# The product with w_out by one level of Strassen over pairs of batches

## The chip, the cores and the metric

The kernel runs on one core of a Trainium2 chip. The metric is the device time of one execution in microseconds, the median of three runs. The engines are named as in the profile: PE is the matrix engine (TensorE), PEld its loading of weights, DVE is VectorE, ACT is ScalarE, POOL is GpSimd; SP is SyncE, which issues most of the transfers, in order.

## What is computed

Three layers follow on each other for 4 batches (B) of 448 tokens (S) and 768 columns (DM): sigmoid attention over 12 heads, a layer with a spatial gate, and a layer that mixes tokens by a complex rotation. The change lies in the second one:

```python
h = np.maximum(x @ w_in, 0.0)                  # 768 -> 1024
u, v = h[..., :512], h[..., 512:]
v_n = (v - mu) / np.sqrt(var + 1e-06)          # over the 512 columns
v_s = np.einsum('ts,bsd->btd', w_spatial, v_n) + b_spatial[None, :, None]
gated = u * v_s
x = gated @ w_out                              # 512 -> 768, goes into the third layer
# third layer
theta = x @ w_theta
y = einsum(w_tok_r, x * cos(theta)) + einsum(w_tok_i, x * sin(theta))
u = x + y
out = u + np.maximum(u @ w_ch, 0.0)
```

## The kernel before, in words

Every product is taken in split precision. A value is kept as a high part, rounded to the matrix engine's format, and a low part, the rest; `mm3` sums three matmuls (high by high, high by low, low by high) into PSUM. Making such a pair takes a copy on ACT (`acopy`) for the high part and a subtraction on DVE (`sub`) for the low part.

The program runs through these stages. **Attention**: 24 rounds in an order that is written out by hand for PE, ACT, DVE and SP. Beside them the weights of the later layers are read, put together from 64-bit values and written back to device memory as 32-bit ones (`Piece`; `f_out` is w_out, `f_th` w_theta, `f_tok` the token weights, `f_ch` w_ch). **First product** (`uv(b, g)`): eight groups for a batch, four for v (`g < 4`) and four for u; each is reduced in a PSUM tile `psd`, copied by ACT with a relu to `ev`, and stored to `v_d` and `u_d`. Some groups run among the rounds, the last ten behind them (`while todo`). The fourth group of v holds the last 64 tokens of two batches. **Spatial product** (`spatial(b, n)`): for each of four chunks `f` of 128 columns of v it makes 11 matmuls into a tile `psp`, multiplies that by the chunk of u on DVE (`gf`, L499) and splits the result into `g`. **Product with w_out** (`project(b, G, d, ps)`): for each of six blocks `d` of 128 output columns, four chunks of 128 of the 512 inner columns times three matmuls into a tile `ppo`; ACT copies it to `x2` and stores it to `x_d`. **Third layer**: the product with w_theta (`pt`), the rotation, the mixing (`py`), and at the end the product with w_ch, which already has the seven-product form that the change brings to w_out (L887).

`ln(b)` loads v of a batch in three transfers (the first 384 tokens, and twice the last 64), takes mean and variance (`bn_stats`, `bn_aggr` on DVE, a power on POOL), scales v on DVE (L468), and splits it into `vh` and `vl`. `prep` loads blocks of a weight into `wq` and splits them. Behind the attention rounds a scheduler sets the order in which each engine's instructions stand; an engine takes its own in that order. PE there has: ten `psd` groups, the spatial products of batches 0 and 1, w_out for batch 0, spatial 2, w_out 1, spatial 3, w_out 2 and 3, theta. PSUM has eight banks; the spatial and the w_out tiles share one pool of six (`ps_2`).

Of the kernel before, what the change touches and what calls it, by code (L numbers as in the profile page):

```python
# [20 lines left out]
DM, DFF = 768, 1024  # L21
# [30 lines left out]
def net(ctx: ExitStack, tc: tile.TileContext, kq, vd, vl, w_in, w_sp, bsp, w_out, w_th, w_tok, w_ch, out):  # L52
# [12 lines left out]
    def mm3(ps, wh, wl, xh, xl, first, last):  # L65
        te.matmul(ps, wh, xh, start=first, stop=False)  # L66
        te.matmul(ps, wh, xl, start=False, stop=False)  # L67
        te.matmul(ps, wl, xh, start=False, stop=last)  # L68

    const = ctx.enter_context(tc.tile_pool(name="const", bufs=1))  # L70
    dram = ctx.enter_context(tc.tile_pool(name="dram", bufs=1, space=DRAM))
# [178 lines left out]
        ve.tensor_copy(xl[b // 2, p][:, :, b % 2, :], X[:, :, L0:S].bitcast(F32))  # L250
        xs[b, p] = X

    def uv(b, g):
        ps = banks("psd")[:, 0, :]
        if g < 4:
            for k in range(KC):
                if g < 3:
                    xh, xlo = (xs[b, k][:, i, g * P:(g + 1) * P] for i in range(2))
                else:
                    xh, xlo = (xl[b // 2, k][:, i].rearrange("p b t -> p (b t)") for i in range(2))  # L260
                te.matmul(ps, xh, wih[:, k, DH:], start=k == 0, stop=False)  # L261
                te.matmul(ps, xh, wil[:, k, DH:], start=False, stop=False)  # L262
                te.matmul(ps, xlo, wih[:, k, DH:], start=False, stop=k == KC - 1)  # L263
            r = x_p.tile([P, DH], F32, tag="ev", name="ev", bufs=2)
            acopy(r, ps, AF.Relu)
            if g < 3:
                nc.scalar.dma_start(v_d[b][g * P:(g + 1) * P, :], r)
            else:
                nc.scalar.dma_start(v_d[b - 1][L0:S, :], r[0:64])
                nc.scalar.dma_start(v_d[b][L0:S, :], r[64:P])  # L270
        else:
            f = g - 4
            fs = slice(f * P, (f + 1) * P)
            for k in range(KC):
                X = xs[b, k]
                mm3(ps[:, :S], wih[:, k, fs], wil[:, k, fs], X[:, 0, :], X[:, 1, :], k == 0, k == KC - 1)
            r = x_p.tile([P, DH], F32, tag="ev", name="ev", bufs=2)
            acopy(r[:, :S], ps[:, :S], AF.Relu)
            nc.scalar.dma_start(u_d[b][fs, :], r[:, :S])

    class Piece:

# [82 lines left out]
    with tc.manual_schedule(engines={mybir.EngineType.PE, mybir.EngineType.Activation, mybir.EngineType.DVE, mybir.EngineType.SP}):  # L365
# [71 lines left out]
        while pieces or loaded or apart or joined:  # L437
            begin_pieces(2)
            end_pieces()
    es_l.close()  # L440


    es_w = ExitStack()
    wb_p = es_w.enter_context(tc.tile_pool(name="wb", bufs=1, reuse_waits="tile"))
    NB = FC * DM + 4 * S
    wbh = wb_p.tile([P, NB], F32R, tag="wbh", name="wbh")
    wbl = wb_p.tile([P, NB], F32R, tag="wbl", name="wbl")
    sph, spl = (w[:, FC * DM:].rearrange("p (c t) -> p c t", c=4) for w in (wbh, wbl))
    woh, wol = (w[:, :FC * DM].rearrange("p (c f) -> p c f", c=FC) for w in (wbh, wbl))
    pxa = es_w.enter_context(tc.tile_pool(name="pxa", bufs=1, reuse_waits="tile"))  # L450
    es_a = ExitStack()
    pw = es_a.enter_context(tc.tile_pool(name="pw", bufs=2, reuse_waits="tile"))
    def ln(b):
        v = pa.tile([P, 4, DH], F32, tag="v", name="v")
        nc.sync.dma_start(v[:, 0:3, :], v_d[b][0:L0, :].rearrange("(c p) f -> p c f", p=P))
        nc.sync.dma_start(v[0:64, 3, :], v_d[b][L0:S, :])
        nc.sync.dma_start(v[64:P, 3, :], v_d[b][L0:S, :])
        st = pa.tile([P, 4, 6], F32, tag="st", name="st")
        mv = pa.tile([P, 4, 2], F32, tag="mv", name="mv")
        for c in range(4):  # L460
            ve.bn_stats(st[:, c, :], v[:, c, :])
            ve.bn_aggr(mv[:, c, :], st[:, c, :])
        ve_ = pa.tile([P, 4], F32, tag="ve", name="ve")
        ve.tensor_scalar_add(ve_, mv[:, :, 1], EPS)
        rs = pa.tile([P, 4], F32, tag="rs", name="rs")
        nc.gpsimd.tensor_tensor(out=rs, in0=ve_, in1=mhalf, op=ALU.pow)
        for c in range(4):
            ve.tensor_scalar(out=v[:, c, :], in0=v[:, c, :], scalar1=mv[:, c, 0:1], scalar2=rs[:, c:c + 1],  # L468
                             op0=ALU.subtract, op1=ALU.mult)
        vh = pa.tile([P, 4, DH], F32R, tag="vh", name="vh")  # L470
        vl = (p2 if b % 2 else pa).tile([P, 3, DH], F32R, tag="vl", name="vl", bufs=1)
        acopy(vh, v)
        sub(vl, v[:, 0:3, :], vh[:, 0:3, :])
        sub(vh[64:P, 3, :], v[64:P, 3, :], vh[64:P, 3, :])
        acopy(vb[b % 2][0:64], v[0:64, 3, :])
        return vh, vl

    U = {}

    def load_u(b):  # L480
        for f in range(FC):
            u = U[b, f] = pa.tile([P, S], F32, tag="u", name="u", bufs=4)
            nc.sync.dma_start(u, u_d[b][f * P:(f + 1) * P, :])

    def spatial(b, n):
        vh, vl = n
        G = []
        for f in range(FC):
            fs = slice(f * P, (f + 1) * P)
            ps = ps_2.tile([P, 512], F32, tag="d", name="psp")  # L490
            o = ps[:, :S]
            for c in range(3):
                te.matmul(o, vh[:, c, fs], sph[:, c, :], start=c == 0, stop=False)
                te.matmul(o, vh[:, c, fs], spl[:, c, :], start=False, stop=False)
                te.matmul(o, vl[:, c, fs], sph[:, c, :], start=False, stop=False)
            te.matmul(o, vh[:, 3, fs], sph[:, 3, :], start=False, stop=False)
            te.matmul(o, vb[b % 2][:, fs], spl[:, 3, :], start=False, stop=True)
            gf = p2.tile([P, S], F32, tag="gf", name="gf")
            ve.tensor_tensor(out=gf, in0=o, in1=U.pop((b, f)), op=ALU.mult)  # L499
            g = pg.tile([P, 2, S], F32R, tag="g", name="g", bufs=6)  # L500
            acopy(g[:, 0, :], gf)
            sub(g[:, 1, :], gf, g[:, 0, :])
            G.append(g)
        return G

    NAMES = ("A11", "A12", "S2", "S1", "S3", "S4", "A22")
    KH = KC // 2
    SUMS = ("S3", "S4")
    f_s = dram.tile([P, KH, len(SUMS), HALF], F32, name="f_s")

    def project(b, G, d, ps):
        ds = slice(d * P, (d + 1) * P)
        for f in range(FC):
# [14 lines left out]
    for i in range(2):  # L528
# [2 lines left out]
        for r in (64, 96):  # L531
            nc.gpsimd.memset(t[r:r + 1].bitcast(F32), 1.0)
        vb.append(t)
    prep(pw, sph, spl, w_sp, 4)
    br = pw.tile([P, S], F32, name="br", bufs=1)
    for r in (64, 96):
        nc.sync.dma_start(br[r:r + 1], bsp)
    bh = pw.tile([P, S], F32R, name="bh", bufs=1)
    nc.gpsimd.memset(spl[64:P, 3, :].bitcast(F32), 0.0)
    ve.tensor_copy(spl[64:65, 3, :], br[64:65])  # L540
    ve.tensor_copy(bh[96:97], br[96:97])
    sub(spl[96:97, 3, :], br[96:97], bh[96:97])
    n0 = ln(0)
    load_u(0)
    prep(pw, woh, wol, f_out, FC)
    while todo:
        uv(*todo.pop(0))
    es_ps.close()
    es_r.close()


    es_ps = ExitStack()
    ps_2 = es_ps.enter_context(tc.tile_pool(name="ps_2", bufs=6, space=PSUM, reuse_waits="tile"))
# [15 lines left out]
    p2 = es_a.enter_context(tc.tile_pool(name="p2", bufs=2, reuse_waits="tile"))  # L569
    G = None  # L570
    for b in range(B):
        Gn = spatial(b, n0)
        if b + 1 < B:
            load_u(b + 1)
            n0 = ln(b + 1)
        if b == 0:
            prep(pw, thh, thl, f_th, KC)
        if b == 1:
            prep(pw, tkh, tkl, f_tok, 7)
        if G is not None and b + 1 < B:  # L580
            for d in range(KC):
                project(b - 1, G, d, ps_2.tile([P, 512], F32, tag="d", name="ppo"))
        if b + 1 < B:
            G = Gn
        else:
            halve(0)
    es_a.close()


    pxb = es_w.enter_context(tc.tile_pool(name="pxb", bufs=2, reuse_waits="tile"))  # L590
    es_b = ExitStack()
    pb = es_b.enter_context(tc.tile_pool(name="pb", bufs=2, reuse_waits="tile"))
# [49 lines left out]
    load_x(0)  # L642
    for n in steps[:2]:
        part_planes(*n)
    split_x(*steps[0])
    join_planes(*steps[0])
    se.activation(warm, XR[steps[0]][:, 0:4], AF.Sin, scale=0.0)
    for b, g in ((B - 2, G), (B - 1, Gn)):
        for d in range(KC):
            project(b, g, d, ps_2.tile([P, 512], F32, tag="d", name="ppo"))  # L650
    es_g.close()
    es_ps.close()

# [147 lines left out]
    with tc.manual_schedule(engines={mybir.EngineType.SP}):  # L801
        for b in range(B):
            for i in range(4):
                for h in range(2):
# [20 lines left out]
                    if i < 3 and (i or b == 2):  # L825
# [175 lines left out]
```

## Time and profile before

| | before |
|---|---|
| median of three runs | 618.04 us (617.21 to 618.92) |
| the profiled execution, first to last instruction | 616.3 us |
| PE busy | 610.3 us (99%) |
| loading of weights on PE | 508.6 us (83%) |
| DVE busy | 414.7 us (67%) |
| ACT busy | 347.2 us (56%) |
| granted clock of PE, mean | 1.000 |

The page of the profile gives the span of the profiled execution alone; the median of the runs is 1.7 us above it. An engine's busy share is a mean over all stages. It doesn't tell whether another engine ever waits for it, nor, for PE, whether a matmul is at its peak, since matmuls overlap and their recorded ends are modelled.

### The profile page before, as it was taken

What the parts mean: (1) busy time and instruction counts of PE and PEld (TensorE: products, weight loads), DVE (VectorE), ACT (ScalarE), POOL (GpSimd) and SP (SyncE); (2) the same over time, 40 slices, a digit from 0 to 9 for tenths busy, and PEclk for the clock granted to TensorE, in tenths of its full rate; (3) what the DMA queues carried; (4) which work ended last, traced back from release to release, by engine and by line L of the source; (5) the groups of instructions that cost most, each with busy time, mean ns of one, the idle gap of its engine ahead of it and who ended that gap; (6) DMA issues with size and microseconds to landing.
All of it is one profiled execution on the core that took longest, in us unless ns stands there. A gap on an engine that the chain in (4) does not pass through costs nothing.

```text
span 616.3 us, 9173 instructions
## 1 busy us (share of the span) xinstructions
PE 610.3 (99%) x3302; PEld 508.6 (83%) x3302; DVE 414.7 (67%) x824; ACT 347.2 (56%) x589; POOL 8.1 (1%) x18
## 2 busy tenths in 40 slices
PE   9999999999999999999999999999999999999997
PEld 4547666856776689999999999999999999999996
DVE  4788577626753557795231497797587787887875
ACT  6896766554656325346236396677376574562540
POOL 0000000000000110000000000000000000000000
PEclk9999999999999999999999999999999999999999
DMA  8758589749864597675867612472085026153503
GB/s 306 275 205 265 180 296 293 243 155 308 271 209 158 178 282 245 192 215 167 224 198 234 188 39 78 90 243 65 27 215 171 26 99 223 60 189 118 213 33 133
DMA packets 83106, 112.62 MB, mean 183 GB/s; under 512 B 27890, under 2 KB 69748, under 8 KB 83060
## 3 DMA queue, kind: packets, MB, share of 16 engines
q1 hardware_dynamic: 74964, 99.00, 50.9%
q10 hardware_dynamic: 8096, 13.03, 6.0%
q8 instruction: 26, 0.43, 0.3%
q14 instruction: 20, 0.16, 0.1%
HBM read 68.06 MB, written 32.93 MB: 164 GB/s over the span
## 4 chain that ended last, share of the span: by engine, by line
PE 93%; DVE 3%; DMA 1%; ACT 1%; issue 1%; SPq 0%; DVEq 0%
PE psa L235 7%; PE py L725 6%; PE py L726 6%; PE py L727 5%; PE pss L206 5%; PE pt L685 5%; PE pt L686 5%; PE pt L684 5%; PE psd L261 3%; PE ppo L67 3%; PE ppo L66 3%; PE ppo L68 3%; PE psd L263 3%; PE psd L262 3%; PE psd L66 3%; PE psd L68 3%
## 5 line engine op out<-in xcount | busy, mean ns | idle before, releaser
L192 ACT ACTIVATE af<-pss,bias 128x896 f32<-128x896 f32 x72 | 66.1, 1022 | 4.9 <-PE pss L202 3.1
L685 PE MATMUL pt<-thl,XT 128*128 128x384 f32 x168 | 56.9, 338 | 0.0
L235 PE MATMUL psa<-af,vr 128*64 128x448 f32 x288 | 56.8, 543 | 0.0
L686 PE MATMUL pt<-thh,XT 128*128 128x384 f32 x168 | 56.8, 338 | 0.0
L684 PE MATMUL pt<-thh,XT 128*128 128x384 f32 x168 | 56.7, 338 | 0.0
L235 PEld LDWEIGHTS psa<-af,vr 128*64 128x64 f32 x288 | 19.6, 137 | 36.3 <-issue 34.7
L63 ACT ACTIVATE ev<-psd 128x448 f32<-128x448 f32 (+1 forms) x30 | 17.0, 567 | 47.5 <-PE psd L263 22.8
L112 DVE SCALAR_TENSOR_TENSOR wq<-wraw,wq 128x384 int32<-128x384 int32 (+2 forms) x51 | 28.7, 594 | 20.7 <-ACT wraw L107 20.6
L66 PE MATMUL psd<-X,wih 128*128 128x448 f32 x96 | 35.7, 372 | 0.0
L68 PE MATMUL psd<-X,wil 128*128 128x448 f32 x96 | 35.2, 367 | 0.2 <-DVE wil L57 0.2
L57 DVE TENSOR_TENSOR X<-psa,X 128x448 fp32r<-128x448 f32 x24 | 14.6, 623 | 30.9 <-ACT X L63 30.9
L67 PE MATMUL ppo<-g,wbh 128*128 128x448 f32 x96 | 35.2, 366 | 0.0
L66 PE MATMUL ppo<-g,wbh 128*128 128x448 f32 x96 | 35.1, 366 | 0.0
L68 PE MATMUL ppo<-g,wbl 128*128 128x448 f32 x96 | 35.1, 366 | 0.0
L67 PE MATMUL psd<-X,wih 128*128 128x448 f32 x96 | 35.1, 366 | 0.0
L107 ACT ACTIVATE wraw<-wraw 128x384 f32<-128x384 f32 (+2 forms) x51 | 29.4, 604 | 9.6 <-DVE wq L100 7.0
L695 ACT ACTIVATE m<-r 128x384 f32<-128x384 f32 x28 | 14.7, 524 | 33.1 <-DVE r L693 33.1
L685 PEld LDWEIGHTS pt<-thl,XT 128*128 128x128 f32 x168 | 31.5, 188 | 0.4
L684 PEld LDWEIGHTS pt<-thh,XT 128*128 128x128 f32 x168 | 31.5, 188 | 0.4
L102 DVE SCALAR_TENSOR_TENSOR wq<-wraw,wq 128x384 int32<-128x384 int32 (+2 forms) x51 | 30.6, 600 | 1.8
L686 PEld LDWEIGHTS pt<-thh,XT 128*128 128x128 f32 x168 | 31.5, 188 | 0.0
L261 PE MATMUL psd<-wih,X 128*128 128x512 f32 x72 | 28.4, 394 | 0.0
(292 smaller groups left out, 1570.3 us busy)
## 6 DMA issues: line engine op xcount, KB each, us to landing
kqr<-in_kq SPq DMA_DIRECT2D x23, 448.0 KB, 4.9
wraw<-in_w_in SPq DMA_DIRECT2D x12, 512.0 KB, 6.1
x_d<-x ACTq DMA_DIRECT2D x24, 224.0 KB, 3.3
xb<-x_d SPq DMA_DIRECT2D x4, 1344.0 KB, 7.4
xp<-xa SPq DMA_DIRECT2D x56, 96.0 KB, 2.5
y_d<-y SPq DMA_DIRECT2D x24, 224.0 KB, 2.0
out_t<-o SPq DMA_DIRECT2D x23, 224.0 KB, 1.9
vr<-in_vd SPq DMA_DIRECT2D x24, 192.0 KB, 5.0
```

The lines of the kernel that those rows point to most:

```text
L66: te.matmul(ps, wh, xh, start=first, stop=False)
L67: te.matmul(ps, wh, xl, start=False, stop=False)
L68: te.matmul(ps, wl, xh, start=False, stop=last)
L192: se.activation(af, ps[:, :, :S], AF.Sigmoid, bias=bias, scale=1.0 / math.sqrt(D))
L206: te.matmul(ps[:, j, :S], t[w][a, 0, c], t[x][a, 1, :], start=n == 0, stop=n == 2)
L235: te.matmul(ps[a, :S], t["v"][:, 2 * c + j, :], t["a"][c][:, j, :], start=False, stop=c == 2)
L261: te.matmul(ps, xh, wih[:, k, DH:], start=k == 0, stop=False)
L684: te.matmul(o, t[:, k, 0, :], thh[:, k, hs], start=k == 0, stop=False)
L685: te.matmul(o, t[:, k, 0, :], thl[:, k, hs], start=False, stop=False)
L686: te.matmul(o, t[:, k, 1, :], thh[:, k, hs], start=False, stop=k == KC - 1)
L725: te.matmul(o, z[:, 0, ds], tkh[:, c, :], start=i == 0 and n == 0, stop=False)
L726: te.matmul(o, z[:, 0, ds], tkl[:, c, :], start=False, stop=False)
```

## The change

Two batches are taken as one pair, b and b+1. Write the gated values, with the 512 inner columns halved, as y0[0], y0[1] (batch b) and y1[0], y1[1] (batch b+1), and w_out as four blocks: rows halved like the inner columns, columns halved at 384. One level of Strassen (in Winograd's form) then takes seven block products instead of eight, of the weights A11, A12, S2, S1, S3, S4, A22 (S1 to S4 are sums of blocks) with B11, B21, T2, T1, T3, B22, T4, in this order on PE. B11 and B21 are the halves of batch b, B22 is one of batch b+1, and T1 to T4 are the differences that four DVE instructions make, in place of the gated values. Each product runs over three blocks `d` of 128 columns, two chunks `c` and three matmuls. Some products are accumulated in a bank that holds an earlier one; others are copied out by ACT (`kept`) and added on DVE to what has been kept (`plus`), which also stores the result through SP.

Around it:
- `spatial` writes its products over u, which is loaded in two transfers a batch into six buffers (`pu`).
- `Norm` scales v on ACT instead of DVE. v of batch 1 is loaded to a place of its own.
- `OutPart` loads the four blocks of one chunk of w_out, splits three, makes S1 to S4 on DVE (four instructions of 384 columns), and splits those. There are two of them.
- The PSUM pools `ps_2` (five banks, with the spatial product) and `ps_a` (three) are opened before the last ten groups of the first product, which use them (`uv_last`).
- Both spatial products of a pair come ahead of its w_out product. The weights of theta and of the token mixing are split at other places, two of them by way of arguments of `project`.
- In the last stage one of the steps that sum w_ch's blocks comes earlier, and the scratch size of the transfers is set.

```diff
 def spatial(b, n):
...
-            gf = p2.tile([P, S], F32, tag="gf", name="gf")
-            ve.tensor_tensor(out=gf, in0=o, in1=U.pop((b, f)), op=ALU.mult)
-            g = pg.tile([P, 2, S], F32R, tag="g", name="g", bufs=6)
-            acopy(g[:, 0, :], gf)
-            sub(g[:, 1, :], gf, g[:, 0, :])
-            G.append(g)
-        return G
+            u = U[b, f // GH][:, f % GH, :]
+            marks['y'] = ve.tensor_tensor(out=u, in0=o, in1=u, op=ALU.mult).ins
+        return [U.pop((b, j)) for j in range(2)]
...
-    def project(b, G, d, ps):
-        ds = slice(d * P, (d + 1) * P)
-        for f in range(FC):
-            mm3(ps[:, :S], woh[:, f, ds], wol[:, f, ds], G[f][:, 0, :], G[f][:, 1, :], f == 0, f == FC - 1)
-        r = pg.tile([P, S], F32, tag="x2", name="x2", bufs=3)
-        acopy(r, ps[:, :S])
-        nc.scalar.dma_start(x_d[b][ds, :], r)
+    def project(b, y0, y1, early, beside):
+        def half(y):
+            t = pg.tile([P, 2, GH, S], F32R, tag="g", name="g", bufs=3)
+            marks['g'] = acopy(t[:, 0], y).ins
+            sub(t[:, 1], y, t[:, 0])
+            return t
...
+        B11, B21 = half(y0[0]), half(y0[1])
+        marks.update({'ya': marks['y'], 'ga': marks['g']})
+        t = pu.tile([P, GH, S], F32, tag="u", name="t1")
+        sub(t, y1[0], y0[0])
+        sub(y0[0], y1[1], t)
+        A = [ps_a.tile([P, 512], F32, tag="a", name="pa_") for d in R3]
+        for d in R3:
+            out_product(A[d], "A11", B11, d, True)
+        p1 = [kept(A[d]) for d in R3]
+        T2 = half(y0[0])
+        E = [ps_2.tile([P, 512], F32, tag="d", name="pb_") for d in R3]
+        for d in R3:
+            out_product(E[d], "A12", B21, d, True)
+            plus(E[d], p1[d], b, d)
+        T1 = half(t)
+        early()
+        sub(y1[0], y1[1], y1[0])
+        sub(y0[1], y0[1], y0[0])
+        for d in R3:
+            out_product(A[d], "S2", T2, d, False)
+        u2 = [kept(A[d]) for d in R3]
+        T3 = half(y1[0])
...
+    with tc.issue_after(last_uv.ins):
+        y0 = spatial(0, N[0])
+        y1 = spatial(1, N[1])
+    project(0, y0, y1, lambda: N.update({2: ln(2)}), lambda: None)
+    load_u(2)
+    N[3] = ln(3)
+    y0 = spatial(2, N[2])
+    load_u(3)
+    with tc.issue_after(marks['ya']), tc.issue_after(marks['ga']):
+        prep(pw, thh, thl, f_th, KC)
+    y1 = spatial(3, N[3])
```

DVE's instructions from the second spatial product on, before. Here `gf` is a gated chunk, `g` its split form, `thl` the low part of w_theta, `vl` and `vh` those of v:

```order
L57 TENSOR_TENSOR g<-gf,g 128x448
L57 TENSOR_TENSOR thl<-wq,thh 128x384 x2
L499 TENSOR_TENSOR gf<-psp,u 128x448 x2
L57 TENSOR_TENSOR vh<-v,vh 64x512
L57 TENSOR_TENSOR g<-gf,g 128x448 x2
L57 TENSOR_TENSOR thl<-wq,thh 128x384 x2
L499 TENSOR_TENSOR gf<-psp,u 128x448 x2
```

The same place in the changed kernel, in the first pair, from the first low half of the gated values (`g<-u`) to that of T2 (the last row). `u<-psp,u` are the multiplies, `t_2714` is T1, and `u<-u` are the sums made in place:

```order
L57 TENSOR_TENSOR g<-u,g 128x896
L525 TENSOR_TENSOR u<-psp,u 128x448
L57 TENSOR_TENSOR g<-u,g 128x896
L57 TENSOR_TENSOR t_2714<-u 128x896
L525 TENSOR_TENSOR u<-psp,u 128x448
L57 TENSOR_TENSOR vh<-v,vh 64x512
L57 TENSOR_TENSOR wtkl<-wq,wtkh 128x448
L525 TENSOR_TENSOR u<-psp,u 128x448
L57 TENSOR_TENSOR thl<-wq,thh 128x384
L57 TENSOR_TENSOR u<-u,t_2714 128x896
L57 TENSOR_TENSOR u<-u 128x896 x2
L57 TENSOR_TENSOR g<-u,g 128x896
```

Each chunk was split on its own behind its multiply; now the sums of both batches stand between the last multiply and the split of T2, with pieces of the second batch pair's v (`vh`) and of later weights (`wtkl`, `thl`) among them.

SP's transfers in the attention rounds, as the difference of the two kernels. `wo` is the staging of `OutPart`, `wraw` a raw weight, `kqr` queries and keys:

```order
 L91 DMA wraw_1096<-in_w_th 128x384
 L91 DMA wraw_1098<-in_w_th 128x384
-L299 DMA f_out_99<-wq_1090 128x384
-L299 DMA f_th_100<-wq_1093 128x384
+L542 DMA wo_2274<-f_out_99 128x384
+L542 DMA wo_2341<-f_out_99 128x384
+L301 DMA f_out_99<-wq_1090 128x384
+L301 DMA f_th_100<-wq_1093 128x384
 L91 DMA wraw_1138<-in_w_th 128x384
 L91 DMA wraw_1140<-in_w_th 128x384
+L542 DMA wo_2341<-f_out_99 128x384
 L175 DMA kqr_1177<-in_kq 128x896
 L175 DMA kqr_1179<-in_kq 128x896
```

Loads of w_out's blocks, which stood behind the rounds, now stand between its stores and the next loads of weights, queries and keys.

## Rows read from the trace of the kernel before

**Rows 1.** The page, first part: busy time of each engine, share of the span, instructions.

```profile
span 616.3 us, 9173 instructions
...
PE 610.3 (99%) x3302; PEld 508.6 (83%) x3302; DVE 414.7 (67%) x824; ACT 347.2 (56%) x589; POOL 8.1 (1%) x18
```

**Rows 2.** The view of waits of PE: in total, times, longest, all in us.

```profile
PE pss L372 <- DVE idle L369: 1.1, 1, 1.1
PE pss L206 <- ACT af L192: 0.8, 2, 0.6
```

**Rows 3.** Windows (us): PE, PEld, DVE, ACT, POOL busy, granted clock, DMA share, GB/s.

```profile
210.60:248.90 38.30, 38.30 (x181) 33.71 (x180) 26.03 (x60) 15.67 (x25) 5.68 (x10) 1.00 0.75 236
...
248.90:343.90 95.00, 95.00 (x468) 87.58 (x467) 44.19 (x77) 42.73 (x74) 2.05 (x2) 1.00 0.69 206
```

**Rows 4.** Timeline of PE around 249 and 343 us: start, duration, instruction.

```profile
249.11 0.36 PE L493 MATMUL psp<-wbh,vh 128*128 128x448 f32 x1
...
343.45 0.37 PE L68 MATMUL ppo<-g,wbl 128*128 128x448 f32 x1
```

**Rows 5.** One tile's instructions, ppo: durations in ns, first and last start.

```profile
L66 PE MATMUL ppo<-g,wbh x96: 358/367/373, 267.0 to 343.0; 128*128 128x448 f32 x96
```

**Rows 6.** Groups of DVE by form: busy us, mean ns of one, idle before.

```profile
L57 DVE TENSOR_TENSOR kql<-kqr,kqh 128x896 fp32r<-128x896 f32 x23 | 25.1, 1092 | 0.8
...
L461 DVE BATCH_NORM_STATS2 st<-v 128x6 f32<-128x512 f32 x16 | 10.3, 675 | 0.8 <-DMA v<-v_d 0.8
...
L499 DVE TENSOR_TENSOR gf<-psp,u 128x448 f32<-128x448 f32 x16 | 9.5, 616 | 0.0
...
L468 DVE TENSOR_SCALAR v<-v,mv,rs 128x512 f32<-128x512 f32 x16 | 7.7, 544 | 4.4 <-POOL rs L466 4.4
L57 DVE TENSOR_TENSOR vl<-v,vh 128x1536 fp32r<-128x1536 f32 x4 | 7.0, 1752 | 3.2 <-ACT vh L63 3.2
...
L57 DVE TENSOR_TENSOR thl<-wq,thh 128x384 fp32r<-128x384 f32 x12 | 6.3, 552 | 1.3 <-ACT thh L63 1.3
...
L57 DVE TENSOR_TENSOR wtkl<-wq,wtkh 128x448 fp32r<-128x448 f32 x7 | 4.4, 625 | 11.9 <-ACT wtkh L63 11.9
...
L57 DVE TENSOR_TENSOR vh<-v,vh 64x512 fp32r<-64x512 f32 x4 | 2.8, 690 | 0.1
```

**Rows 7.** Groups of ACT by form, the same columns.

```profile
L192 ACT ACTIVATE af<-pss,bias 128x896 f32<-128x896 f32 x72 | 66.1, 1022 | 4.9 <-PE pss L202 3.1 <-PE pss L206 1.8
...
L63 ACT ACTIVATE ev<-psd 128x512 f32<-128x512 f32 x14 | 8.4, 597 | 23.2 <-PE psd L263 22.8 <-ACT ev L63 0.5
...
L63 ACT ACTIVATE vh<-v 128x2048 fp32r<-128x2048 f32 x4 | 7.6, 1904 | 4.4 <-DMA wq<-f_out 4.4
...
L63 ACT ACTIVATE wbh<-wq 128x384 fp32r<-128x384 f32 x8 | 4.0, 520 | 6.3 <-DMA wq<-f_out 6.3
```

**Rows 8.** Timeline around 210 us, where the last ten groups begin.

```profile
209.98 0.62 DVE L57 TENSOR_TENSOR X<-psa,X 128x448 fp32r<-128x448 f32 x1 [0.48 <-ACT X L63]
...
210.61 0.47 PE L66 MATMUL psd<-X,wih 128*128 128x448 f32 x1
```

**Rows 9.** Timeline of SP in the attention rounds.

```profile
97.75 0.33 SPq L299 DMA_DIRECT2D f_out<-wq  x1
...
102.62 0.33 SPq L175 DMA_DIRECT2D kqr<-in_kq  x1
```

**Rows 10.** DMA issues: KB each, median us from issue to landing.

```profile
u<-u_d SPq DMA_DIRECT2D x16, 224.0 KB, 3.8
...
f_out<-wq SPq DMA_DIRECT2D x8, 192.0 KB, 3.6
...
v<-v_d SPq DMA_DIRECT2D x8, 128.0 KB, 4.0
...
v_d<-ev ACTq DMA_DIRECT2D x4, 128.0 KB, 4.3
```

**Rows 11.** Timeline of ACT's queue: the last store of v.

```profile
236.39 0.49 ACTq L269 DMA_DIRECT2D v_d<-ev  x1
```

More of the change, by code (lines that the diff above doesn't have):

```diff
@@ L67, in mm3 @@
         te.matmul(ps, wh, xl, start=False, stop=False)
-        te.matmul(ps, wl, xh, start=False, stop=last)
+        return te.matmul(ps, wl, xh, start=False, stop=last)
     const = ctx.enter_context(tc.tile_pool(name="const", bufs=1))
@@ L279, in uv @@
             nc.scalar.dma_start(u_d[b][fs, :], r[:, :S])
+        return ins
     class Piece:
@@ L478, in net @@
+    def ln(b):
+        n = Norm(b)
+        n.stats()
+        n.scale()
+        n.split()
+        return n
     U = {}
     def load_u(b):
-        for f in range(FC):
-            u = U[b, f] = pa.tile([P, S], F32, tag="u", name="u", bufs=4)
-            nc.sync.dma_start(u, u_d[b][f * P:(f + 1) * P, :])
+        for j in range(2):
+            u = U[b, j] = pu.tile([P, GH, S], F32, tag="u", name="u")
+            nc.sync.dma_start(u, u_d[b][j * GH * P:(j + 1) * GH * P, :].rearrange("(c p) t -> p c t", p=P))
@@ L509, in net @@
     f_s = dram.tile([P, KH, len(SUMS), HALF], F32, name="f_s")
[L511 to L517 removed]
+    WO = {n: [w[:, i] for w in (woh, wol)] for i, n in enumerate(("A11", "A12", "A22", "S3", "S2", "S4", "S1"))}
@@ new lines, in net, with out_product, kept, put @@
+    marks = {}
+    def project(b, y0, y1, early, beside):
[4 more added lines that the diff above has]
+            return t
+        def out_product(ps, n, Y, d, first):
+            ds = slice(d * P, (d + 1) * P)
+            h, l = WO[n]
+            for c in range(GH):
+                for i, (w, j) in enumerate(((h, 0), (h, 1), (l, 0))):
+                    te.matmul(ps[:, :S], w[:, c, ds], Y[:, j, c, :], start=first and c == 0 and i == 0,
+                              stop=c == GH - 1 and i == 2, skip_group_check=not first)
+        def kept(ps):
+            r = pg.tile([P, S], F32, tag="x2", name="x2", bufs=8)
+            acopy(r, ps[:, :S])
+            return r
+        def put(q, i, d, r):
+            q.dma_start(x_d[i][d * P:(d + 1) * P, :], r)
+        def plus(ps, r, i, d):
+            add(r, ps[:, :S], r)
+            put(nc.sync, i, d, r)
+        R3 = range(KH)
+        B11, B21 = half(y0[0]), half(y0[1])
[20 more added lines that the diff above has]
+        T3 = half(y1[0])
+        E = [ps_2.tile([P, 512], F32, tag="d", name="pe_") for d in R3]
+        for d in R3:
+            out_product(E[d], "S1", T1, d, True)
+        p5 = [kept(E[d]) for d in R3]
+        B22 = half(y1[1])
+        for d in R3:
+            out_product(A[d], "S3", T3, d, False)
+            plus(A[d], p5[d], b + 1, d + KH)
+        T4 = half(y0[1])
+        beside()
+        for d in R3:
+            out_product(E[d], "S4", B22, d, False)
+            plus(E[d], u2[d], b + 1, d)
+        for d in R3:
+            out_product(A[d], "A22", T4, d, False)
+            put(nc.scalar, b, d + KH, kept(A[d]))
@@ L568, in net @@
     pg = es_g.enter_context(tc.tile_pool(name="pg", bufs=2, side="right", reuse_waits="tile"))
[L569 to L586, printed above, removed]
+    pu = es_g.enter_context(tc.tile_pool(name="pu", bufs=6, side="right", reuse_waits="tile"))
+    load_u(0)
+    load_u(1)
+    with tc.issue_after(last_uv.ins):
[9 more added lines that the diff above has]
+    y1 = spatial(3, N[3])
     es_a.close()
+    pxa = es_w.enter_context(tc.tile_pool(name="pxa", bufs=1, reuse_waits="tile"))
+    halve(0)
     pxb = es_w.enter_context(tc.tile_pool(name="pxb", bufs=2, reuse_waits="tile"))
@@ L644, in net, with begin_theta @@
         part_planes(*n)
[L645 to L650, printed above, removed]
+    def begin_theta():
+        split_x(*steps[0])
+        join_planes(*steps[0])
+        se.activation(warm, XR[steps[0]][:, 0:4], AF.Sin, scale=0.0)
+    project(2, y0, y1, lambda: prep(pg, tkh, tkl, f_tok, 7), begin_theta)
     es_g.close()
```

144 lines of the change are left out of this document (96 added, 48 removed).

## The prediction

> **What bounds the kernel now.** I read the busy times first. TensorE (PE) is busy for 610.3 of the 616.3 us [rows 1], so the reader should ask next whether any other engine is ever waited for. The view of PE's waits answers it: its largest entries are 1.1 us at the very start and 0.8 us in two pieces [rows 2], both far ahead of the part that is changed. The windows then show that part: from 248.9 to 343.9 us (the spatial product and the product with w_out) PE is busy for all 95.00 us at a granted clock of 1.00, VectorE (DVE) for 44.19, ScalarE (ACT) for 42.73 [rows 3]. So a matmul taken out of this stage shortens the run by its place in PE's stream, as long as what feeds the rest stays in time.
>
> That place is read from starts, not from durations. The first spatial matmul starts at 249.11, the last one of the w_out product at 343.45 [rows 4]. Between them lie 16 groups of 11 spatial matmuls and 24 groups of 12 for w_out, 464 in all, so (343.45 - 249.11) / 463 = 0.2038 us from one to the next. The recorded duration of one is 367 ns [rows 5]: neighbours overlap, and durations would count each column of time nearly twice.
>
> **What is removed.** Before, the product needs 4 batches x 6 column blocks x 4 chunks x 3 = 288 matmuls. After, each of two batch pairs needs 7 products x 3 blocks x 2 chunks x 3 = 126, in all 252. 36 x 0.2038 = **7.34 us** less. Against the profiled span that is 616.3 - 7.3 = 609.0; the median of the runs is 618.04, 1.7 us above that span, and I carry this offset along: 618.04 - 7.34 = 610.7 if nothing waits.
>
> The Trainium skill ("TensorE: Matmul & The Clock Gate", section "Back-to-back issue gap") gives a warm matmul N / 2.4 GHz plus about 2.5 ns, for 448 columns 189 ns. By it the gain is an estimated 36 x 0.189 = 6.8 us. The starts above say 204, so the measured pitch stands.
>
> **What is added on DVE.** Prices are those of like forms [rows 6]: 1.092 us for a subtraction over 128x896, 0.616 for one over 128x448 out of PSUM. Low halves: 14 x 1.092 in place of 16 of half the size, 15.3 - 9.9 = +5.4. Block sums: 8 x 1.092 = +8.7. Adds of a product to a kept one: 18 x 0.616 = +11.1. The scaling of v goes to ACT: 16 x 0.544 = -8.7. Sum +16.5, so about 61 of the remaining 87.7 us. On ACT the high halves are at most 14 x 1.022 us more [rows 7], about 57 of 87.7. Neither becomes the bound by its sum. The 8 block sums and 6 more blocks of w_out lie before 248.9, where DVE is busy for 26.03 and ACT for 15.67 of 38.3 us [rows 3]; they cost nothing while that idle time covers them, and at most a late start of the spatial product if not.
>
> The scaling on ACT has no row: 128x512 with two per-row operands. The bounds are 0.597 (a copy of 128x512) and 1.022 (128x896 with one such operand) [rows 7]; being nearest in size to the former I take 0.7. The Trainium skill ("ScalarE: Activation LUTs") has 280 ns + 0.833 ns a column with a pointer operand and some 93 ns for a second, an estimated 0.80 us here; no run so far shows it, and it speaks against the move by 0.4 us for a batch of four.
>
> **Where PE can now be made to wait.** The excerpt of DVE's order shows it. In the first pair PE runs the 44 spatial matmuls of batch 1, then A11 and A12 (36), and then S2, which needs T2, the third sum split. In DVE's row T2 stands behind batch 2's normalised v, and its high half may be written only when batch 0's spatial product is through. From that moment: ACT's copy 1.904 [rows 7]; then on DVE [rows 6] vl 1.752, four multiplies 4 x 0.616, two low halves 2 x 1.092, one sum 1.092, vh 0.690, one block each of two weights 0.625 and 0.552, three sums 3 x 1.092, T2's low half 1.092: 13.7 us. Together 15.6. PE has (44 + 36) x 0.2038 = 16.3 us of work. The margin is 0.7 us; handing over from ACT to DVE and from DVE to PE is not in it (0.01 us from the end of a read to PE's start in [rows 8]). I take a wait of 0.3 us, with nothing and 1 us as bounds. In the second pair only a multiply, three sums and the low half, 5.0 us, face the 36 x 0.2038 = 7.3 us of A11 and A12: no wait.
>
> **The handover ahead of it.** The last products of the first layer now use the new PSUM pools, whose first bank is free when DVE has read X. That read starts at 209.98 and takes 0.62, and PE starts at 210.61 because of it already [rows 8]. I take 0.1, at most one more such read, 0.6.
>
> **SyncE's queue (SP) in the attention rounds.** Eight loads of w_out's blocks and three of v now stand there, as the second excerpt shows; each w_out load waits until its store has landed, 3.6 us [rows 10]. The store is issued at 97.75, so the load holds SP until about 101.4; its next own wait, a load of queries and keys, is issued at 102.62 [rows 9]. So I take 0.1. If a landing takes twice as long, 7.2, SP is free at 105.3 only, 2.7 us too late, and the splits of queries and keys that PE's scores wait for are late by as much: 2.7 is the upper bound, nothing the lower.
>
> Moving the other preparations and one step of the last stage changes no count on PE, and the same idle time of DVE and ACT hides it. Sum: -7.34 + 0.3 + 0.1 + 0.1 = -6.84, **611.2 us**.
>
> **Rivals.**
> *T2 late because of batch 2's statistics* (chance 0.18). The last rows of v for batch 2 are stored by ACT, at 236.39 before [rows 11], land 4.3 later, and are loaded in 4.0 [rows 10]: 244.7. Statistics 4 x 0.675 and four scalings bring it to about 251 to 254, against 249.1 + 44 x 0.204 = 258.1, when the copy may start anyway: 4 us to spare or more. For it speaks that the scaling of batches 0 and 1 (8 x 0.6 to 1.0) and six more blocks of w_out (6 x 0.520 = 3.1) now stand ahead of that store on ACT, 8 to 11 us; against it that ACT is idle for 22.6 of the 38.3 us around. If all of it delays the store, PE loses up to 7 us, if the idle time takes most of it, none. Between, 2.5: 618.04 - 7.34 + 2.5 = 613.2.
>
> *SP's queue late in the rounds* (0.06): 610.7 + 2.7 = 613.4.
>
> *The durations are right after all* (0.03): 36 x 0.367 = 13.2, 604.8. Against it stands that 464 x 0.367 = 170 us do not fit into 95. The Trainium skill's "Trainium Kernel Development and Optimization" calls matmul busy time a bad metric since matmuls are pipelined; by that rule, the trace agrees.
>
> *The gain is eaten* (0.08): the rival on batch 2 at its full 7 us, 617.7, no change that can be told.
>
> *Slower* (0.05). The load of batch 2's last rows on SP waits for the store, and the loads of the gated half u stand behind it. If they are late, no spatial product can be multiplied, the five banks fill, and PE stops. The store's 4.3, u's 3.8 [rows 10] and a multiply of 0.6 must be over by 249.1 + 5 x 11 x 0.204 = 260.3, so the store may leave at 251.6. Before it left at 236.39, 15 us earlier. A loss begins there, and the run is slower than before by over 0.3% (1.85 us, about what a measurement of this kernel can tell from no change) only from 15 + 7.3 + 1.9 = 24 us of delay. Delayed by 30 us, it would end at 624.
>
> **How the numbers follow.** The likeliest case, waits of 0 to 1 us plus the small terms, has 0.60 and reaches from 610.0 to 612.5. Below it the durations' case holds 0.03, above it the waits of 1 to 4 us 0.24. The range from 609.7 to 614.6 takes in the bounds of T2 and SP and leaves the eaten gain, the slower case and the durations' case out. Faster: 0.60 + 0.03 + nearly all of 0.24, 0.86; same 0.09; slower 0.05.
>
> **What the profile after would show.** Right: the matmuls from the first spatial one to the last of w_out number 428 and keep a pitch of 0.204, so about 87.2 us; PE's waits there sum to under 1 us; what there is stands at S2 of the first pair and is put down to DVE's split of T2; the attention rounds have the waits of before. Wrong would be the prediction if PE waits for several us at S2 or at the later products behind ACT's or DVE's splits, if the first layer's products or the rounds grow longer, or if the stage that follows starts later than the stage that precedes it has become shorter.

## The result, and the profile after

The changed kernel took 612.71 us, the median of four runs (612.18 to 613.15), beside 618.13 for the kernel before (four runs, 617.21 to 618.92). The ratio is 0.9914, with a 95% interval from 0.99 to 0.9928. The forecast was 611.2, with a range from 609.7 to 614.6: the time lies in it, and 1.5 us above the number.

The page of the profiled execution, its first part:

```profile
span 611.2 us, 9106 instructions
...
PE 603.5 (99%) x3266; PEld 501.8 (82%) x3266; DVE 437.9 (72%) x840; ACT 363.2 (59%) x599; POOL 9.9 (2%) x18
```

PE is still busy for nearly all of the span, which is 5.1 us shorter [rows 1]. The next view is the waits of PE; they are to be read beside [rows 2]:

```profile
PE pss L206 <- ACT af L192: 1.7, 1, 1.7
PE pss L374 <- DVE idle L371: 1.1, 1, 1.1
PE pe__3285 L574 <- DVE g L57: 0.7, 1, 0.7
PE pss L202 <- DMA kqr<-in_kq: 0.3, 1, 0.3
```

The wait of 1.1 us at the start is that of before. New is an entry on `pe__3285`, a bank of the product with w_out, and the wait for ACT's `af`, early in the attention rounds, has grown from 0.8 to 1.7. The windows of the three stretches from the last ten groups of the first product on (the same columns as in [rows 3]) show where the time went:

```profile
211.70:250.20 38.50, 38.50 (x182) 33.92 (x181) 29.86 (x56) 22.51 (x29) 7.28 (x9) 1.00 0.43 139
250.20:338.76 88.56, 87.80 (x430) 80.26 (x428) 62.57 (x97) 51.69 (x79) 2.23 (x2) 1.00 0.71 221
338.76:611.20 272.44, 268.99 (x1387) 254.17 (x1385) 210.45 (x436) 154.81 (x300) 0.00 (x0) 1.00 0.41 125
```

Three differences of starts make up the 5.1 us:

| stretch | before | after | difference |
|---|---|---|---|
| start to the first spatial matmul | 249.11 [rows 4] | 250.20 | +1.09 |
| from there to the start of the last w_out matmul | 94.34 [rows 4] | 88.35 | -5.99 |
| from there to the end | 272.85 | 272.67 | -0.18 |

The stretch that is changed gave 5.99 instead of 7.34 us. The 1.35 us are in PE's timeline (start, duration, instruction; in brackets idle time and its releaser), in the second pair:

```profile
328.65 0.36 PE L574 MATMUL pa__3169<-g,wbl 128*128 128x448 f32 x1
329.12 0.67 PE L574 MATMUL pa__3170<-g,wbh 128*128 128x448 f32 x2
...
330.44 0.41 PE L574 MATMUL pe__3285<-g,wbh 128*128 128x448 f32 x1
331.51 0.47 PE L574 MATMUL pe__3285<-g,wbh 128*128 128x448 f32 x1 [0.66 <-DVE g L57]
```

The starts of neighbours lie 0.204 apart elsewhere. From 328.65 to 329.12 it is 0.47, from 330.44 to 331.51 it is 1.07, and the start behind each such wait comes 0.1 later than the pitch: 0.26 + 0.11 + 0.87 + 0.11 = 1.35. The reader should ask what ACT and DVE did just then. ACT's timeline (`g` is the high part of an operand of the product, `x` a copy out of PSUM; `XT`, `xr` and the table load are theta's first step, the beginning of the next layer):

```profile
316.03 0.94 ACT L63 ACTIVATE g<-t 128x896 fp32r<-128x896 f32 x1
321.98 1.59 ACT L63 ACTIVATE XT<-xb 128x768 fp32r<-128x768 f32 x2 [5.00 <-DMA xb<-x_d]
323.47 0.94 ACT L63 ACTIVATE g<-u 128x896 fp32r<-128x896 f32 x1
...
327.13 1.28 ACT L777 ACT_TABLE_LOAD   x1
...
328.54 0.53 ACT L63 ACTIVATE x<-pa__3170 128x448 f32<-128x448 f32 x1
...
329.38 0.95 ACT L63 ACTIVATE g<-u 128x896 fp32r<-128x896 f32 x1
```

ACT stands for 5.00 us until the load `xb` has landed. Queued behind are the high part of T3 (323.47), two copies `xr` and a table load, the copy out of `pa__3170` (328.54), for which PE waits until 329.12, and the high part of B22 (329.38). From that DVE makes the low part (330.37, 1.09 us), for which PE waits until 331.51. DVE stands there, too:

```profile
322.86 0.96 DVE L57 TENSOR_TENSOR XT<-xb,XT 128x768 fp32r<-128x768 f32 x1 [3.88 <-ACT XT L63]
...
330.37 1.09 DVE L57 TENSOR_TENSOR g<-u,g 128x896 fp32r<-128x896 f32 x1 [3.97 <-ACT g L63]
```

Ahead of the load on SP stands a transposing transfer that holds the queue for 5.44 us:

```profile
308.72 5.44 SPq L634 DMA_TRANSPOSE xa<-x_d  x1
314.28 0.51 SPq L766 DMA_DIRECT2D xb<-x_d  x1
```

In the first pair, where the prediction put the wait, there is none. T2's low half starts on DVE at 272.80, and S2 begins on PE at 275.45, right behind its forerunner:

```profile
272.80 1.09 DVE L57 TENSOR_TENSOR g<-u,g 128x896 fp32r<-128x896 f32 x1
```

```profile
275.45 0.57 PE L574 MATMUL pa__2717<-g,wbh 128*128 128x448 f32 x2
```

So the margin was 275.45 - 273.89 = 1.56 us, not 0.7. The last store of v is the row that answers to [rows 11]; it leaves ACT 11.1 us later than before, and batch 2's scaled v (four instructions from 255.73) is done at 258.67, 0.5 us before the copy that waits for PE to free its buffer:

```profile
247.48 0.47 ACTq L270 DMA_DIRECT2D v_d<-ev  x1
...
255.73 2.94 ACT L486 ACTIVATE v<-v,ve,rs 128x512 f32<-128x512 f32 x4 [0.85 <-DVE ve L484]
259.21 1.92 ACT L63 ACTIVATE vh<-v 128x2048 fp32r<-128x2048 f32 x1 [0.54 <-PE psp L522]
```

### The profile page after: what moved, and what is told of

Its sections match the earlier page's. It is cut to its first block, busy times and chain, and to the rows that moved or that the text cites. A ratio compares the mean times of both kernels' runs of the same rounds, so it can differ in the third digit from the quotient of the medians.

```text
span 611.2 us, 9106 instructions
## 1 busy us (share of the span) xinstructions
PE 603.5 (99%) x3266; PEld 501.8 (82%) x3266; DVE 437.9 (72%) x840; ACT 363.2 (59%) x599; POOL 9.9 (2%) x18
## 4 chain that ended last, share of the span: by engine, by line
PE 89%; DMA 4%; DVE 3%; ACT 1%; SPq 1%; issue 1%; DVEq 0%; ACTq 0%
PE psa L235 8%; PE py L853 6%; PE pss L206 6%; PE py L854 6%; PE py L855 6%; PE pt L813 5%; PE pt L814 5%; PE pt L812 5%; PE psd L262 3%; PE psd L66 3%; PE psd L264 3%; PE psd L263 3%; PE psd L68 3%; PE psd L67 3%; PE psp L520 1%; PE psp L519 1%
## 5 line engine op out<-in xcount | busy, mean ns | idle before, releaser
L100 DVE TENSOR_SCALAR wq<-wraw 128x384 int32<-128x384 uint32 (+2 forms) x51 | 19.3, 378 | 14.9 <-DMA wraw<-in_w_th 7.9
L206 PE MATMUL pss<-kqh 64*128 64x448 f32 x138 | 27.5, 395 | 1.8 <-ACT af L192 1.7
L63 ACT ACTIVATE xr<-xp 128x768 uint16<-128x768 uint16 x28 | 28.8, 1069 | 0.0
```

Source lines behind the costliest of these rows:

```text
L63: return se.activation(o, a, f)
L206: te.matmul(ps[:, j, :S], t[w][a, 0, c], t[x][a, 1, :], start=n == 0, stop=n == 2)
```

## The experiments

Theory W: PE's 1.35 us in the second pair come from ACT and DVE waiting for the load of x, with splits queued behind. Theory D, the rival: DVE's added sums and adds are too long for the cover. No experiment leaves part of the computation out; one does a product twice, one makes a sum five times. The kernel before is timed beside each on the same chip, 618.2 to 618.4 us.

### Theta's first step behind the split of T4

```diff
     def begin_theta():
-        split_x(*steps[0])
-        join_planes(*steps[0])
-        se.activation(warm, XR[steps[0]][:, 0:4], AF.Sin, scale=0.0)
+        with tc.issue_after(marks['g']), tc.issue_after(marks['l']):
+            split_x(*steps[0])
+            join_planes(*steps[0])
+            se.activation(warm, XR[steps[0]][:, 0:4], AF.Sin, scale=0.0)
```

The marks are the copy and the subtraction of T4's split.

> The first step of theta (copies of x to XT and xr, the table load) stands behind the split of T4 on ACT and DVE. Theory W: in the changed kernel PE loses 1.35 us in the second pair because ACT and DVE wait for the load of x (xb) with the splits of T3 and B22 queued behind. Then the waits of PE there go, the stretch from the first spatial to the last w_out matmul falls from 88.35 to 87.0 to 87.3 us, and the time from 612.7 to about 611.4. Theory D: the block sums and adds on DVE are too long for the cover, theta's step has no part in it; then the stretch stays at 88.3 and the time at 612.7. If the step comes too late for theta, a new wait of PE stands at the first pt.

The stretch from the first spatial to the last w_out matmul fell to 87.03 us (249.22 to 336.25), without a wait: 427 steps of 0.2038. That is what W forecast. But the time was 613.07 us (ratio 0.9919, 0.9906 to 0.9932), no gain on the changed kernel. The view of waits says where it went:

```profile
PE pt L813 <- DVE r L820: 1.8, 1, 1.8
```

The 1.8 us stand not at the first theta tile, as the expectation had as a chance, but at the fourth, at 347.9: PE has two theta banks, and DVE had not yet read the second tile. DVE had waited 3.06 us for a load of w_ch ahead of that read; the next experiment shows the same wait.

### The load of x ahead of the transposing transfer

```diff
-    halve(0)
...
     load_x(0)
+    with tc.issue_after(marks['x']):
+        halve(0)
```

The mark is the load of x; `halve` issues the transposing transfer.

> Only the order of two transfers on SP changes: the load of x (xb) is issued ahead of the transposing transfer that holds SP for 5.4 us; DVE's row stays the same. Theory W: xb lands some 5 us earlier, at about 316.5, ACT no longer waits for it, and PE's waits in the second pair shrink from 1.35 to 0.3 us or less; time 611.4 to 611.8. Theory D: nothing changes, 612.7.

The stretch was 87.02 us, with DVE's row unchanged up to there: D falls, since the same sums and adds now fit. ACT's wait for the load is down from 5.00 to 1.28 us, and it ends 4.07 us earlier:

```profile
317.91 1.59 ACT L63 ACTIVATE XT<-xb 128x768 fp32r<-128x768 f32 x2 [1.28 <-DMA xb<-x_d]
```

But ACT's row is another: the copies `xr` and the table load, which stood ahead of the high part of B22, now stand behind the last split, as they do in the first experiment. So these two runs show that theta's first step made PE wait; they don't tell the wait for its load from its own work on ACT. The time was 613.86 us (0.9918, 0.9905 to 0.993), where 611.4 to 611.8 was expected, again with a new wait:

```profile
PE pt L813 <- DVE r L820: 1.2, 1, 1.2
```

SP's timeline shows the edit, and further down a load of w_ch (`wq`):

```profile
311.61 0.38 SPq L765 DMA_DIRECT2D xb<-x_d  x1
312.16 8.44 SPq L634 DMA_TRANSPOSE xa<-x_d  x1
...
335.90 0.67 SPq L910 DMA_DIRECT2D wq<-f_ch  x1
```

DVE waits for that load with its read of the second theta tile (L820) behind it:

```profile
345.36 0.36 DVE L60 TENSOR_TENSOR wq<-wq 128x192 f32<-128x192 f32 x1 [2.45 <-DMA wq<-f_ch]
...
347.36 0.56 DVE L820 SCALAR_TENSOR_TENSOR r<-m,pt 128x384 f32<-128x384 f32 x1
```

The load landed 9.4 us after its issue. So the second wait is a load that DVE's row comes to in order, as the first one was. In the changed kernel PE comes to theta 1.7 us later, and the load, issued at 337.85, lands in 5.5 us, so that it is there in time. Why it takes 9.4 us here is not shown.

### Both edits of order: the load of x first, and the sums of w_ch as before

The condition for the sums of w_ch's blocks is a part of the change that the prediction put at nothing in passing. Here it is undone.

```diff
-                    if i < 3 and (i or b == 2 or (b, h) == (0, 1)) and len(done) < 18:
+                    if i < 3 and (i or b == 2):
                         sums_ch(len(done))
```

> The load of x ahead of the transposing transfer, as in the run before, and the condition of the sums of w_ch's blocks as in the kernel before (no step at the first batch's second half). Theory W2: what the earlier load gave back in the second pair (1.33 us) was lost at the third product of theta, where DVE waits 2.45 us for a load of w_ch (wq) with the reads of the second theta tile queued behind it, so that PE gets no free bank (wait 1.4 us). Then this wait goes as well: from the first theta matmul to the end 272.4 to 272.6 us instead of 274.0, span 609.6 or less, time 611.0 to 611.6. Rival: the loss lies in theta's own chain (copy, rotation and reads by ACT and DVE, which start only when PE has made the first tile), then the wait stays at 1.2 to 1.6 us and the time at 612.7 to 613.5.

It took 611.04 us (0.9883, 0.987 to 0.9896). All waits of PE that are left lie ahead of the spatial product:

```profile
PE pss L206 <- ACT af L192: 1.2, 1, 1.2
PE pss L374 <- DVE idle L371: 1.1, 1, 1.1
PE pss L206 <- DVE X L57: 0.3, 1, 0.3
PE psd L68 <- DVE wil L57: 0.2, 1, 0.2
```

```profile
250.04:337.27 87.23, 87.23 (x429) 80.38 (x428) 63.24 (x98) 52.20 (x79) 2.23 (x2) 1.00 0.66 211
```

87.23 us busy out of 87.23, and 272.50 from the first theta matmul to the end: W2 held (the wait that it speaks of stood at the fourth theta tile), and this kernel beats both others.

### The sums of w_ch as before, alone

> The changed kernel with the condition of the sums of w_ch's blocks alone as before. Theory W2: in the changed kernel the load of w_ch has landed when DVE comes to it, since PE, held up in the second pair, comes 2 us later; so nothing changes: waits of 1.35 us in the second pair, 272.5 us from the first theta matmul to the end, time 612.4 to 613.0. If the earlier sum were worth something by itself, the end would come later.

This expectation fell: 621.1 us (1.0048, 1.0034 to 1.0061), slower than before the change. It is the wait of the kernel with the load of x first, for the same load, made worse. SP:

```profile
340.38 6.71 SPq L634 DMA_TRANSPOSE xa<-x_d  x1
347.14 0.66 SPq L909 DMA_DIRECT2D wq<-f_ch  x1
```

Issued a step later, the load of w_ch now stands behind a second transposing transfer (6.71 us). DVE, whose row still has the sum ahead of its read of the second theta tile (L819), waits 6.43 us for it:

```profile
351.53 0.36 DVE L60 TENSOR_TENSOR wq<-wq 128x192 f32<-128x192 f32 x1 [6.43 <-DMA wq<-f_ch]
...
353.52 0.56 DVE L819 SCALAR_TENSOR_TENSOR r<-m,pt 128x384 f32<-128x384 f32 x1
```

PE stood for 5.2 us and then ran at little more than half its pace for a while:

```profile
348.60 0.34 PE L814 MATMUL pt<-thh,XT 128*128 128x384 f32 x1
354.13 0.69 PE L812 MATMUL pt<-thh,XT 128*128 128x384 f32 x1 [5.20 <-DVE r L819]
354.62 0.52 PE L813 MATMUL pt<-thl,XT 128*128 128x384 f32 x1
354.94 0.52 PE L814 MATMUL pt<-thh,XT 128*128 128x384 f32 x1
```

The theta matmuls then start 0.32 apart instead of 0.176, thirteen times. From the first theta matmul to the end it was 280.56 us instead of 272.44. In the experiment ahead, with the same order of the two transfers, the sum stands further back in DVE's row; DVE waits 3.39 us for the load at 355.10, and PE for nothing. So the earlier sum is not worth nothing: beside the late load of x it is worth 8 us, and with the early load of x it costs 1.5 (274.02 and 272.50 from the first theta matmul to the end).

### The product S1 by T1 twice

```diff
             out_product(E[d], "S1", T1, d, True)
+            out_product(E[d], "S1", T1, d, True)
```

> The kernel with theta's step behind the split, and the product S1 by T1 made twice (the second time over the first, into the same banks): 18 matmuls more for a pair, 36 in all, and nothing more on the other engines. By the pitch of 0.204 us between starts it is 7.3 us slower than that kernel, about 618.7; by the recorded durations (0.367 us) 13.2 us, 624.6.

It took 619.77 us (1.0024, 1.0013 to 1.0036), 6.7 us more than the kernel it is made from; the stretch grew from 87.03 to 94.36 us, and 7.33 / 36 = 0.2036 us a matmul. Theta's wait was 1.1 us instead of 1.8, which is a part of the difference between 6.7 and 7.33. The durations' 13.2 us are out. By the formula of the Trainium skill ("TensorE: Matmul & The Clock Gate", section "Back-to-back issue gap") for a single warm matmul, 189 ns and 6.8 us for 36 are an estimate; the trace differs from it and decides.

### No early loads of w_out and of v

```diff
+    with tc.issue_after(stored['s']):
+        N[1] = Norm(1, pwo)
+        wo = [OutPart(pwo, 0), OutPart(pwo, 1)]
...
-    wo = [OutPart(pwo, 0)]
-    N[1] = Norm(1, pwo)
...
-    wo.append(OutPart(pwo, 1))
```

The mark is the last store of the rounds on SP.

> The loads of w_out's blocks and of batch 1's v leave SP's row in the attention rounds and stand behind the last store there. If these loads cost the rounds what the trace shows at 110 us (0.3 us of PE's lead lost where queries and keys are loaded 2 us later), that shift of 0.3 us between 100 and 112 us is gone, and the time is 0.3 us shorter unless the later loads delay the tail, which the windows would show. Rival: the shift is chance, as the 0.9 us at 30 us must be (both kernels have the same instructions up to there), and stays or wanders.

The rounds ran without the shift of 0.3 us, but so did those of eight of the ten profiled kernels that keep the early loads; it was 0.3 us in the changed kernel and 0.7 in one other. The time was 620.86 us (1.0045, 1.0028 to 1.0061), for another reason: the later loads put ACT's and DVE's work in another order, and the prediction's rival on batch 2's statistics came true. DVE:

```profile
256.67 0.69 DVE L476 BATCH_NORM_STATS2 st<-v 128x6 f32<-128x512 f32 x1 [2.41 <-DMA v<-v_d]
...
264.09 1.76 DVE L57 TENSOR_TENSOR vl<-v,vh 128x1536 fp32r<-128x1536 f32 x1 [4.94 <-ACT vh L63]
265.77 2.74 DVE L527 TENSOR_TENSOR u<-psp,u 128x448 f32<-128x448 f32 x5
```

The last rows of v leave ACT at 249.75 (before: 236.39 [rows 11]) and land late; the statistics, the scaling and the copy follow; and the multiplies stand in DVE's row behind `vl`, which waits for ACT. Five PSUM banks fill, and PE stops. That is the end that the slower rival described, by another way: the store was in time for u by that rival's own bound (251.6), and DVE waited not for u but for the copy of v:

```profile
260.15 0.37 PE L525 MATMUL psp<-spl,vb 128*128 128x448 f32 x1
266.44 0.74 PE L521 MATMUL psp<-sph,vh 128*128 128x448 f32 x1 [5.92 <-DVE u L527]
```

```profile
260.30:266.40 6.10, 0.22 (x2) 0.00 (x0) 2.31 (x3) 4.25 (x5) 0.00 (x0) 0.83 0.90 334
266.40:271.40 5.00, 4.96 (x14) 4.43 (x15) 3.55 (x6) 3.66 (x6) 0.00 (x0) 0.53 0.00 0
```

After it had stood for 5.92 us, PE's granted clock was 0.53 for the next 5.0 us, that is, mostly the lower of its two levels (1.2 GHz), and 14 matmuls took the time of 25. Waits in the second pair came on top.

### Four more sums ahead of T2

```diff
-        sub(t, y1[0], y0[0])
+        for _ in range(1 if b else 5):
+            sub(t, y1[0], y0[0])
```

> The sum that makes T1 is made five times instead of once in the first pair (the same values each time). By the order, 3.9 us more of DVE work stand ahead of the low half of T2 (four sums 4.37, two adds 1.24 moved ahead, one sum 1.09 and one weight 0.62 moved behind). The margin worked out ahead (0.7 us) lets PE wait 3.2 us at S2 of the first pair, the margin in the trace (T2 ready at 273.9, S2 begins at 275.45: 1.56 us) 2.3 us.

615.97 us in a single run. T2's low half was done at 276.77, 27.23 us behind the first spatial matmul, where the changed kernel has 23.69: 3.5 us of work more, as meant. But the scheduler answered on PE as well and put matmuls of T1's product and of batch 2's spatial product between those of T2, so that PE lost only 0.8 us in the first pair. The margin isn't measured by this; it stands on the trace alone.

```profile
275.69 1.08 DVE L57 TENSOR_TENSOR g<-u,g 128x896 fp32r<-128x896 f32 x1
```

### The scaling of v on DVE again

```diff
-            ve.scalar_tensor_tensor(out=mr, in0=self.mv[:, :, 0], scalar=-1.0, in1=rs, op0=ALU.mult, op1=ALU.mult)
...
-                se.activation(v[:, c, :], v[:, c, :], AF.Identity, bias=mr[:, c:c + 1], scale=rs[:, c:c + 1])
+                ve.tensor_scalar(out=v[:, c, :], in0=v[:, c, :], scalar1=mv[:, c, 0:1], scalar2=rs[:, c:c + 1],
+                                 op0=ALU.subtract, op1=ALU.mult)
```

> The scaling of v is made on DVE again, as before the change. In the changed kernel the last store of v leaves ACT at 247.5, 11 us later than before the change, and batch 2's scaled v is ready 0.4 us before its buffer is free. Theory: 6 us of ACT work ahead of that store go away, the store leaves at 241 to 243, u is loaded 4 to 6 us earlier; but DVE has 2.2 us more ahead of T2 for batch 2, which the earlier loads cover. PE's waits in the first pair stay at zero, so the time stays at 612.7 (612.2 to 613.2). Rival: DVE is so full in the first pair that the 2.2 us of batch 3's scaling delay a split, and PE waits 0.5 to 2 us there.

612.39 us (0.9914, 0.9901 to 0.9927), the changed kernel's time. There was no wait in the first pair. The part is neutral: the second half of the last store of v left ACT at 241.47 instead of 247.98, and PE waited for neither. PE's waits were again in the second pair, 2.6 us of them in the profiled execution, which was the longest of the four (614.60).

### Repeats

> The changed kernel once more, beside the next one on the same chip: 612.4 to 613.2 us. From the first spatial to the last w_out matmul 88.3 us or somewhat more (its wait in the second pair was 1.3 to 2.5 us in the runs that left that place as it is).

> The kernel with the load of x ahead of the transposing transfer and the sums of w_ch at their old place, once more: 610.6 to 611.5 us, some 1.6 us under the changed kernel; no wait of PE between the first spatial matmul and the end; 87.0 us from the first spatial to the last w_out matmul.

> The kernel before, for a second profile of it. Theory: the 0.5 to 1.5 us by which the profiles differ at 30 us (30.05 in the profile before, 30.1 to 31.5 in those of the other kernels) are chance in the landing of the first loads, since the instructions up to there are the same; then this profile too may lie anywhere from 30.0 to 31.5. Rival: the change delays something there; then this profile stands at 30.0 to 30.1 again.

On one chip the changed kernel took 613.52 us (0.9918, 0.9902 to 0.9935) and the kernel with both edits of order 612.25 (0.9894, 0.9879 to 0.9909), 1.3 us less; their stretches were 88.61 and 87.03 us. The two medians lie 0.8 and 1.2 us above those of the other chips and above what was expected, and the intervals overlap a little here. The second profile of the kernel before has the matmul of 30 us at 29.86, outside the range given for chance and nearer to the rival.

### The kernel before with the scratch size

> The kernel before with the scratch size of the transfers that the change sets, and nothing else. In two profiles of the kernel before, the matmul that waits for ACT in the second round starts at 30.05 and 29.86 us, and the loads of v (vr) of the first 31 us land in 5.2 and 4.8 us; in eleven of kernels with the change at 30.1 to 31.5 (mean 30.7) and in 5.7 to 6.6. If the scratch size does it, this kernel stands at 30.3 to 31.3, its vr loads land in 5.7 us or more, and it is 0.3 to 0.9 us slower than before. If it is where the change puts its data, or chance, it stands at 29.8 to 30.2, 5.2 us or less, and the time is that of before.

It stood at 30.65 us, with the loads of v landing in 5.6, and took 618.67 us, the time of before (1.0004, 0.9994 to 1.0015). The first mark is where the scratch size was to put it, the second lies between the two cases, and the times cannot tell 0.3 us. This stays open.

## Why the prediction was right, and by how much it was off

**PE as the bound, and the size of the gain.** Right. 36 matmuls at the pitch of starts are 7.34 us; the stretch without waits is 7.32 us shorter (94.34 to 87.02), and putting 36 back costs 7.33.

**DVE and ACT don't become the bound by their sums.** Right: DVE is busy for 62.57 and ACT for 51.69 of the 88.56 us (forecast 61 and at most 57). The scaling on ACT, for which 0.7 was taken, is 0.805:

```profile
L486 ACT ACTIVATE v<-v,ve,rs 128x512 f32<-128x512 f32 x16 | 11.9, 805 | 3.8 <-DMA wq<-in_w_sp 2.0 <-DVE ve L484 1.9
```

By the Trainium skill ("ScalarE: Activation LUTs", section "What ACT_TABLE_LOAD costs"), whose rule on pointer operands gave an estimate of 0.80, the trace agrees.

**The wait at T2.** Forecast 0.3, measured none; the working left out how far neighbouring DVE instructions overlap. From the start of ACT's copy (259.21) to the end of T2's low half (273.89) it took 14.68 us instead of 15.6. A row of 2.09 us covers two sums of 1.09 each.

**"In the second pair ...: no wait."** This is the step that failed, by 1.35 us in the changed kernel and 1.6 in its repeat (88.61 - 87.03). The working counted DVE's instructions for T2 alone, and T2 was in time there too. It left out theta's first step, which begins among the second pair's products, stands in the same rows of ACT and DVE as the splits of T3 and B22, and waits for a load. In the kernel before ACT stood for the same load, and until nearly the same time, with little queued behind that PE needed; now each product needs a split from it:

```profile
322.34 0.85 ACT L63 ACTIVATE XT<-xb 128x768 fp32r<-128x768 f32 x1 [2.43 <-DMA xb<-x_d]
```

That it's theta's step, and not DVE's sums and adds, is shown by the two orders that move the step or its load: no wait with the same sums. How much of the 1.35 us is the wait for the load (5.00 us of ACT) and how much the step's own work on ACT ahead of B22's high part (`xr` 1.07 and 1.08, the table load 1.28) is not shown, since both orders moved that work too. That it may count is seen in the kernel with four more sums, where PE waits 1.12 us for a copy (333.38) that stands behind the table load (331.97).

**"Moving the other preparations and one step of the last stage ..."** Right on PE's count, wrong on idle time hiding the step of the last stage wherever it stands, though in the changed kernel this did not show. The earlier step of w_ch's sums moves its load ahead of a transposing transfer. Without it the changed kernel is 8 us slower.

**The handover and SP's queue.** Forecast 0.1 each. The handover is 0.05 (a gap of 0.31 instead of 0.26 us over the pitch). The shift in the rounds is 0.3 and 0.7 us in two profiles with SP's early loads and nothing in eight, 0.1 in the mean.

**The start.** The first spatial matmul starts 1.09 us later in the profile and 0.2 in its repeat (249.32); the sum had 0.2 for the handover and SP. By 31 us a matmul that waits for ACT already starts 1.15 later. In eleven profiles of kernels with the change it starts at 30.1 to 31.5, in two of the kernel before at 29.9 and 30.1, though the instructions up to there are the same. The first spatial matmul starts at 249.2 to 250.4 in the eleven, in the mean 0.7 us later than in the two (248.93 and 249.11). The two profiles of the changed kernel alone differ by 0.88, so that chance is a large part of one profile's number; whether the change adds half a microsecond is open.

**The rivals.** Batch 2's statistics came within 0.5 us of costing time. The store was late by all of the 11 us that the prediction gave as the worst case; it landed in 2.3 us instead of 4.3, the load of its rows took 2.6 instead of 4.0, and three of the four statistics were done before this load landed; together that took up the delay. With somewhat more delay, in the kernel without early loads, this rival occurred, and the run was slower than before.

**The range.** Its upper end was made for a wait of 1 us at T2 and for 2.7 us of SP's queue. The first didn't occur, the second was 0.1 in the mean. What took their room, theta's step in the second pair and the later start, was not in the working, so that the time lies in the range is in part luck.

## What to carry to other kernels

When matmuls are taken out of a stage that PE bounds, price them by the distance of their starts, and then look at who now stands close behind PE: each engine that has become a supplier must be read instruction by instruction in order, with every transfer that its row comes to. A wait for a load that cost nothing while the engine mostly drained results can cost time once PE waits for that engine's next split: here ACT's 5.00 us, with the work queued behind, became 1.35 us of PE. Try repairs of such waits together as well as alone, and read the trace after each: here the first repair uncovered the next wait at once, and of two edits one alone gave nothing, the other alone cost 8 us, and both together gained 1.3 to 1.7.

## What the runs showed of the hardware that was not expected

A wait of PE can cost more than its length. After waits of 5.9 and 5.2 us the granted clock fell (0.53 in the 5.0 us behind the first, 0.51 in the 4.9 us behind the second; matmuls 0.37 and 0.32 apart instead of 0.204 and 0.176), which cost 2.2 us more each time. Behind the wait of 0.87 us in the changed kernel the pitch was 0.204 again after one matmul, at a granted clock of 1.00.

The transposing transfer holds SP's queue while it is issued, for 5.2 to 8.4 us in these profiles, and what stands behind it is issued only then: in the changed kernel the load of x at 314.28, with the two in the other order at 311.61.
